# A fused attention and relu-squared MLP kernel: the second group's query and key loads wait for the first values load, and the first 185 steps stand in another order

## The chip, the cores and the metric

The kernel runs on one core of a Trainium2 chip. The metric is the device time of one execution in microseconds (us); before the change it is 211.09 us, the median of 3 runs (210.98 to 211.52). A core has five engines that each work through their own program in order: TensorE (PE in the profile; its weight loads are PEld), VectorE (DVE), ScalarE (ACT), GpSimd (POOL) and SyncE (SP), which here only issues DMAs.

## The reference

Attention over 4 batches of 8 heads, 768 tokens and 64 channels, in which each query sees the first 4 keys (the sinks) and the last 128 keys up to itself; then a two-layer MLP on the heads put side by side, 3072 tokens by 512 channels.

```python
keep = (pos[None, :] < n_sink) | ((rel >= 0) & (rel < window))
a = softmax(where(keep, q @ k.T / sqrt(D), -1e9))
x = (a @ v).transpose(0, 2, 1, 3).reshape(B * S, H * D)   # 3072 x 512
h = x @ w_in                                              # 512 x 2048
r = maximum(h, 0)
out = (r * r) @ w_out                                     # 2048 x 512
```

## The kernel before

Tokens lie in tiles of 128. Batch 0 is worked in three groups of two tiles: group 0 is tokens 0 to 255, group 1 tokens 256 to 511, group 2 the rest; the texts below call group 1 the second group. For a group, four loads bring keys and queries as fp32, 256 KB each: two for the keys and two for the queries, each for four heads (`m` = 0 or 2 counts pairs of heads). `load_qk` (L332, the DMA at L350) issues them on SP, but group 0's queries on ACT. From each load one **cast** makes bf16 (`qs<-qr`, in the helper `copy`: L192 on ACT, L194 on DVE). TensorE transposes it (`pt<-ident,qs`, L503), and one copy takes the result out of PSUM (`qkT<-pt`). Then come, per group, the scores (`ps`, L609; in group 0 with a matmul at L602 that adds the mask), the exponentials (`expm<-ps`, L630, ACT), the mask over the window's edges (L642 on DVE by a product with `tri`, or L218 on POOL by a select), the sinks' scores (`pk`, L568, and `es`, L576), the values product (`po`, L678), and the norm: a reciprocal and a product on DVE (L694, L695), two instructions for each quarter. The **bridge** turns the result over for the MLP (`px<-ident,xn_sb`, L727, copied to `xT`). **Layer 1** (L762) multiplies `xT` with w_in, four blocks of 128 columns at a time into PSUM `pm`; relu and square follow on ACT and DVE, and layer 2 later.

w_in is loaded in four quarters of 512 KB (`load_w_in`, L307), w_out in four too (L315), the values in tiles of 128 tokens, two to a call (`load_v`, L380, 128 KB a tile, converted on the way), group 2's and batch 1's keys and queries as bf16 (`load_cast`, L371). All of these are issued by POOL and go over one queue, q0 in the profile, which takes them in order of issue. SP's loads go over q1, ACT's over q10. `load_sinks` (L423) brings the sink tokens' values of one batch (8 KB) on SP, and POOL spreads them over heads once they are there (`vs<-vs_in,head_rows`, L550, four instructions).

Nothing in the kernel decides the order at run time. Every step is created as an `Op` with a number that counts up in the order of creation, and the text table `ORDER` lists these numbers in the order in which the steps are issued; a letter behind a number picks the engine (p, d, a, g for PE, DVE, ACT, POOL), and `+0` or `+1` picks one of the two PSUM pools. Each engine works its share of the list in that order. The numbers of the loads come from the list of load calls near the end of the kernel (L1289 to L1312), so a moved call changes the numbers of others.

`DUMMIES` gives some steps a number of **idle passes**: 128x128 matmuls of `ident` on itself (`warm`, L185), whose result the step's own passes overwrite, or at the start `pw<-tri` (`warmup`, L1372). Before the change they are 29 at the start, 31 and 24 ahead of two of group 0's transposes, and 3 or 4 at three later steps: 95 passes.

`behind` in a load call makes a load wait until another has landed (`after_dma`, L208). `yields` is a hint to the planner which made the table, and has no effect on the instructions.

Of the kernel before, what the change touches and what calls it, by code (L numbers as in the profile page):

```python
# [18 lines left out]


ORDER = """
990 1 0 2 7 8 9 10 11 12 13 14 15 16 17 18 56a 991+0 55d 61a 3 60d 57+1 62+0 19 20 59a 5 6 58d 4 65 63d 67+0 21 64a
75+1 69 89d 22 77 23 76+0 68+0 24 25 70 71+1 88d 73 93d 90+0 78 79+1 72 94a 81 74 83+0 92d 100+1 91a 80 102 82 95+0 66
97d 26 85 110+1 101+1 96d 103g 104 84d 98+0 27 86d 152+0 105g 99 112 111+0 153 114 115g 106+1 113d 28 29 116+1 108
160+0 107 117 154a 30 109 118 119 161 120+1 121a 31 122 168+1 123d 169 32 33 34 155a 170a 162d 172+1 331 164+0 176+0
171d 163a 165 35 166d 36 167d 156+1 173 157 177 174d 124+1 158a 37 38 125a 126d 39 180+1 127+0 332 133+1 181 129d 178a
128a 136 130+1 179d 282+1 182d 334 131 141+1 132+0 140+1 183d 283 40 144 142 137g 284 285 41 145d 159d 143d 134 146+1
135d 147 286 138+1 287 288 278 139 42 43 148+0 175a 150 149d 151d 289 44 279 184+1 290 185 193+0 280 281 200+0 201 291
194 45 204+1 196+0 202 46 203 205 198a 186 197 207a 293 206 187+0 199a 216+0+0 47 48 195a 217 49 188d 234+1+0 50 235
190+0 219 208+0 87 292 237 209 295 191 218 297+0 189 220 51 336 52 212 53 210a 294 211 255+0 252+1 254 299 298 256 54  # L30
253a 257 444 223+0+1 333 238d 445 192a 226 304 213 224 221+0 312 222 300 241+1+0 301 214+0 296 244 215 302 225 446
# [26 lines left out]
985 967d 969 983 984 989 986 988 987  # L58
"""
DUMMIES = {  # L60
    57: 31, 62: 24, 75: 4, 85: 3, 110: 4, 991: 29,
}


# [53 lines left out]
def kernel(  # L118
# [58 lines left out]
    def bank(slot, name, shape, dtype):  # L177

        return rooms[slot.pool][slot.room].tile(shape, dtype, name=name, tag=f"{slot.pool}{slot.room}")
# [105 lines left out]
    def dma_op(queue, name, run, us, behind=None, takes=(), yields=()):  # L285

        def go(e):
            ds = run(e)
            if behind is not None:
                for d in ds:  # L290
                    after_dma(d, loaded[behind])
            loaded[name] = ds[-1]
        o = op(-5, {queue: (0.9 if queue == "pool" else 0.5) + (0.3 if behind else 0.0)}, go, dma=us, takes=takes,
               follow=[chained[queue]] if queue in chained else (),
               after=[ops[behind]] if behind is not None else ())
        ops[name] = chained[queue] = o
        o.yields += [ops[y] for y in yields]
        o.follow += [ops[y] for y in yields]
        return o
# [3 lines left out]
    def load_w_in(i, behind=None, yields=()):  # L303
        c = slice(512 * i, 512 * i + 512)
        w_in_op[i] = dma_op(
            "pool", ("w_in", i),
            lambda e: [nc.gpsimd.dma_start(out=w_in_sb[:, i],  # L307
                                           in_=moe_w_in[:, c].rearrange("(a p) f -> p a f", p=128))],
            2.6, behind, yields=yields)
        w_in_op[i].margin = 0.4 + 0.4 * i  # L310
# [21 lines left out]
    def load_qk(b, m0, ti, g, pairs=2, behind=None, yields=()):  # L332


        t0, n = GROUPS[b][g]
        shares = 4 // pairs if n == 2 else 2 if pairs == 1 else 1
        half, share = m0 // pairs % shares, ("share", b, g, ti, m0 // (pairs * shares))
        if not half:
            qr_slot[share] = Slot("qr", 4 if n == 2 and pairs == 1 else 2)
        for m in range(m0, m0 + pairs):  # L340
            qr_slot[b, m, ti, g] = qr_slot[share]

        def run(e):
            if half == 0:
                qr_t[share] = bank(qr_slot[share], "qr", [128, shares * 2 * pairs, n * D], FP32)
            t = qr_t[share][:, 2 * pairs * half:2 * pairs * half + 2 * pairs, :]
            qr_t[b, "all", m0, ti, g] = t
            for m in range(m0, m0 + pairs):
                qr_t[b, m, ti, g] = t[:, 2 * (m - m0):2 * (m - m0) + 2, :]
            return [(nc.sync if ti or g else nc.scalar).dma_start(  # L350
                out=t,
                in_=(q, k)[ti][b, 2 * m0:2 * m0 + 2 * pairs, t0:t0 + 128 * n, :].rearrange(
                    "h (p t) d -> p h (t d)", t=n))]
        o = dma_op("sp" if ti or g else "act", ("qk", b, m0, ti, g), run, 16 * pairs * ROW[256 * n] + (0.7 if (b, m0, ti, g) == (0, 0, 0, 0) else 0.0), behind,
                   () if half else [qr_slot[share]], yields)
        for m in range(m0, m0 + pairs):
            ops["qk", b, m, ti, g] = o
# [18 lines left out]
    def load_v(b, s, behind=None, yields=()):  # L376

        for t in (2 * s, 2 * s + 1):
            def run(e, t=t):
                return [nc.gpsimd.dma_start(  # L380
                    out=v_sb[b % 2][:, t, :, 0:D],
                    in_=v[b, :, 128 * t:128 * t + 128, :].rearrange("h p d -> p h d"))]
            o = dma_op("pool", ("v", b, t), run, 0.9, behind if t == 2 * s else None, (), yields)
            o.after.append(c_rest if b else c_fill)
        ops["cast", b, s] = o
# [35 lines left out]
    def load_sinks(queue, b):  # L421
        eng = nc.scalar if queue == "act" else nc.sync
        dma_op(queue, ("vs_in", b), lambda e: [eng.dma_start(out=vs_in[:, b, 0:D], in_=v[b, :, 0:NSINK, :])], 0.1)  # L423
# [862 lines left out]
    NATURAL, TURNED, BIASED = (2, 3), (), 1  # L1286
    FAST = {1: ((0, 1), (2,)), 2: ((0,), (1, 2)), 3: ((0,), (1, 2))}
    CLASSIC2 = ((0, 0),)
    for g in range(2):  # L1289
        for m in (0, 2):  # L1290
            for ti in (1, 0):
                load_qk(0, m, ti, g)
            if m and not g:
                load_sinks("sp", 0)
    for b in range(1, B):
        load_sinks("sp", b)
    load_v(0, 0, None, [("qk", 0, 2, 0, 1)])
    load_w_in(0)
    load_v(0, 1)
    for i in range(1, 4):  # L1300
# [109 lines left out]
```

## Time and profile before

| | |
|---|---|
| median of 3 runs | 211.09 us |
| profiled execution | 209.94 us |
| its span, first to last instruction | 208.2 us |
| PE busy | 200.9 us (96%) |
| DVE busy | 178.0 us (85%) |
| ACT busy | 131.6 us (63%) |
| POOL busy | 98.6 us (47%) |
| q0, the software queue | 12.59 MB, 82.7% of 16 DMA engines' span |

All durations below are from the one profiled execution; microseconds count from the start of its span. A row of a timeline gives the start, the time that it takes, the engine, the line in the kernel, the operation with output and input, the shapes and the count of alike instructions; in brackets stands how long the engine was idle just before, and what ended that. "SPq" and "ACTq" are issues of DMAs on these engines. [...] A row of the table of stretches gives from:to, the length, the busy time of PE, PEld, DVE, ACT and POOL with the number of instructions, then the granted clock, the DMA share and the GB/s.

### The profile page before, as it was taken

The numbers are of one execution on the slowest core, as the hardware profiler recorded it, in microseconds if no ns is written. First come the engines' busy times: TensorE is split into PE (matmuls) and PEld (weight loads), VectorE is DVE, ScalarE is ACT, GpSimd is POOL, SyncE is SP. The second block draws the span as 40 slices with busy tenths as digits, with TensorE's granted clock in tenths as the row PEclk, the third lists the DMA queues.
The fourth block names the chain that finished last, engine by engine and source line by source line (L and its number), as shares of the span: only waits on it lengthen the run. The fifth ranks groups of instructions, "written<-read, shape, count | busy, mean of one in ns | idle before, by whom it ended". The sixth has DMA issues, their size and how long they took to land.

```text
span 208.2 us, 6087 instructions
## 1 busy us (share of the span) xinstructions
PE 200.9 (96%) x2535; PEld 177.6 (85%) x2535; DVE 178.0 (85%) x343; ACT 131.6 (63%) x205; POOL 98.6 (47%) x141
## 2 busy tenths in 40 slices
PE   7979999999899999999999999999999999999993
PEld 7757997579878889889878988998889999999893
DVE  5385767989999998999998888999989998998853
ACT  2678428718988168899888448989871452584010
POOL 7767983899489936989523529000280000000000
PEclk9999999999999999999999999999999999999999
DMA  5999999999999999999999995901023220200205
GB/s 162 218 216 202 184 186 213 177 155 179 148 61 118 156 137 241 92 188 154 129 138 229 108 136 152 159 0 25 4 50 127 57 82 22 101 0 3 99 5 201
DMA packets 96043, 26.12 MB, mean 125 GB/s; under 512 B 86800, under 2 KB 93456, under 8 KB 96016
## 3 DMA queue, kind: packets, MB, share of 16 engines
q0 software_dynamic: 69248, 12.59, 82.7%
q1 hardware_dynamic: 25568, 12.49, 28.6%
q10 hardware_dynamic: 1200, 0.66, 1.1%
q8 instruction: 20, 0.33, 0.6%
q14 instruction: 7, 0.06, 0.1%
HBM read 27.30 MB, written 6.29 MB: 161 GB/s over the span
## 4 chain that ended last, share of the span: by engine, by line
PE 76%; DVE 10%; DMA 6%; ACT 5%; issue 1%; ACTq 0%
PE py L1239 25%; PE pm L892 25%; PE pm L762 9%; DMA qr<-in_q_dram 6%; PE po L678 5%; PE ps L609 4%; PE py L990 3%; PE py L1100 2%; PE pt L503 1%; DVE sg L1213 1%; DVE xn_sb L695 1%; DVE r L942 1%; ACT gT_sb L915 1%; ACT qkT L192 1%; DVE gT_sb L1213 1%
## 5 line engine op out<-in xcount | busy, mean ns | idle before, releaser
L630 ACT ACTIVATE expm<-ps 128x1024 bf16<-128x1024 f32 (+1 forms) x48 | 44.1, 953 | 10.0 <-PE ps L609 8.9
L218 POOL TENSOR_SCALAR_AFFINE_SELECT expm<-expm 128x512 bf16<-128x512 bf16 x38 | 26.5, 730 | 46.9 <-ACT expm L630 21.5
L942 DVE CUSTOM_DVE_ANT_0 r<-pm,t 128x512 bf16<-128x512 f32 x54 | 36.0, 684 | 1.6 <-PE pm L892 1.2
L1239 PEld LDWEIGHTS <-gT_sb 128*128 128x128 bf16 x320 | 30.4, 98 | 4.5 <-issue 0.9
L892 PEld LDWEIGHTS <-w_in_sb 128*128 128x128 bf16 x384 | 32.5, 114 | 1.7 <-issue 1.5
L192 ACT ACTIVATE t<-pm 128x512 f32<-128x512 f32 x42 | 24.7, 600 | 13.4 <-PE pm L892 12.7
L192 ACT ACTIVATE osb<-py 128x256 f32<-128x256 f32 (+1 forms) x36 | 14.0, 397 | 19.9 <-PE py L1239 15.0
L892 PEld LDWEIGHTS <-wi 128*128 128x128 bf16 x288 | 24.7, 114 | 0.8 <-issue 0.7
L1239 PEld LDWEIGHTS <-sg 128*128 128x128 bf16 x240 | 22.5, 98 | 3.1 <-DVE sg L1213 0.3
L762 PE MATMUL pm<-xT,w_in_sb 128*128 128x256 bf16 x192 | 22.7, 273 | 0.4 <-DVE xT L194 0.4
L892 PE MATMUL pm<-xs,wi 128*128 128x256 bf16 (+1 forms) x192 | 21.6, 246 | 0.0
L892 PE MATMUL pm<-xs,w_in_sb 128*128 128x256 bf16 (+1 forms) x192 | 21.5, 246 | 0.0
L762 PEld LDWEIGHTS <-w_in_sb 128*128 128x128 bf16 x192 | 20.5, 114 | 1.1 <-issue 0.8
L1239 PE MATMUL py<-wt,gT_sb 128*128 128x256 bf16 x160 | 20.7, 273 | 0.2
L1239 PE MATMUL py<-wt,sg 128*128 128x256 bf16 x160 | 20.8, 273 | 0.0
L1239 PE MATMUL py<-w_out_sb,gT_sb 128*128 128x256 bf16 x160 | 20.4, 273 | 0.0
L915 ACT ACTIVATE gT_sb<-r 128x1024 bf16<-128x1024 bf16 x17 | 18.0, 1057 | 1.8 <-DVE r L942 1.6
L678 PE MATMUL po<-v,expm 128*128 128x65 bf16 x352 | 18.0, 193 | 0.5 <-ACT expm L630 0.3
L678 PEld LDWEIGHTS <-expm 128*128 128x128 bf16 x352 | 16.8, 97 | 1.8 <-ACT expm L630 0.5
L695 DVE TENSOR_TENSOR xn_sb<-po,rc 128x512 bf16<-128x512 f32 (+1 forms) x28 | 17.2, 615 | 1.0
L1253 DVE TENSOR_TENSOR osb<-py,osb 128x256 f32<-128x256 f32 x30 | 12.1, 415 | 4.7 <-PE py L1239 4.6
L609 PE MATMUL ps<-qkT 64*128 64x128 bf16 (+1 forms) x256 | 14.5, 238 | 0.9 <-ACT expm L630 0.6
(108 smaller groups left out, 382.2 us busy)
## 6 DMA issues: line engine op xcount, KB each, us to landing
out_dram<-osb SPq DMA_DIRECT2D x11, 512.0 KB, 3.4
v<-in_v_dram POOLq DMA_DIRECT2D x24, 128.0 KB, 6.3
qn<-in_k_dram POOLq DMA_DIRECT2D x20, 128.0 KB, 6.6
qn<-in_q_dram POOLq DMA_DIRECT2D x20, 128.0 KB, 6.2
w_in_sb<-in_moe_w_in_dram POOLq DMA_DIRECT2D x4, 512.0 KB, 9.4
w_out_sb<-in_moe_w_out_dram POOLq DMA_DIRECT2D x4, 512.0 KB, 10.0
qr<-in_k_dram SPq DMA_DIRECT2D x4, 256.0 KB, 6.8
qr<-in_q_dram ACTq DMA_DIRECT2D x2, 256.0 KB, 4.1
```

Of the source, the lines that this page charges most:

```text
L192: return nc.scalar.activation(out=dst, in_=src, func=AF.Copy)
L218: nc.gpsimd.affine_select(out=e_tile, in_=e_tile, compare_op=ALU.is_ge, fill=fill, base=i - 1, pattern=[[0, n], [1 if i else -1, 128]], ch ...
L609: nc.tensor.matmul(ps[:, h2, o:o + w], lhsT=qkT_sb[r, m, 1, c, :], rhs=qkT_sb[r, m, 0, qb:qb + w // 128, :], start=(i == 0 and not biased) ...
L630: nc.scalar.activation(out=x[:, :, o:512], in_=bank_t["s", b, s, m][:, :, o:512], func=AF.Exp, scale=scale)
L678: touch(("po", b, s, m0), e, nc.tensor.matmul(pv[:, i, h2, :], lhsT=lhsT, rhs=rhs, start=(n_ == 0), stop=(n_ == len(mms) - 1)), j)
L695: touch(("po", b, s, m0), e, nc.vector.tensor_tensor(out=xn_sb[:, 2 * s:2 * s + 2, 128 * (m0 + j0):128 * (m0 + j0 + nj)].rearrange("p i (j ...
L762: nc.tensor.matmul(pm[:, i, :], lhsT=w_in_sb[:, fb // 4, kb, fb % 4:512:4], rhs=xT[:, c0 // 256:(c0 + cw) // 256, kb, :], start=(kb == 0), ...
L892: touch(tag, e, nc.tensor.matmul(y[:, bk, i, :], lhsT=weights(name, f0 + i, a), rhs=rhs[:, a, :], start=fresh and i == 0 and a == 0, stop= ...
L915: nc.scalar.activation(out=d, in_=x, func=AF.Square)
L942: touch(tag, e, nc.vector._custom_dve(TENSOR_ADD_SAT, out=d.rearrange("p n c -> p (n c)"), in0=T["y"][:, 1].rearrange("p n c -> p (n c)"), ...
L1239: touch((b, u), e, nc.tensor.matmul(region(name), lhsT=x[:, i, :], rhs=w_[:, i, :], start=first and i == 0, stop=i == HB - 1, skip_group_c ...
L1253: ins = nc.vector.tensor_tensor(out=d, in0=region(of), in1=d, op=ALU.add)
```

## The change

Three things are edited. **The load list**: the four loads of group 1's keys and queries come after the first values load, and the first of them (keys, heads 0 to 3) is told to wait until the first values tile has landed (`behind=("v", 0, 0)`). The sink loads of all four batches thereby come ahead of them on SP. **The order**: 185 steps at the start of `ORDER` are listed in another order; everything after them is as before. **The idle passes**: 57 and 62 (ahead of group 0's transposes) get 9 and 14 instead of 31 and 24, others 3 to 5: 68 passes instead of 95.

```diff
 ORDER = """
-990 1 0 2 7 8 9 10 11 12 13 14 15 16 17 18 56a 991+0 55d 61a 3 60d 57+1 62+0 19 20 59a 5 6 58d 4 65 63d 67+0 21 64a
+990 1 0 2 7 8 9 10 11 56d 60a 55d 991+0 3 15 57+0 61d 62+1 16 59a 12 64d 13 14 17 18 19 20 5 67+1 6 75+0 58d 88d 89d
...
 DUMMIES = {
-    57: 31, 62: 24, 75: 4, 85: 3, 110: 4, 991: 29,
+    57: 9, 62: 14, 75: 4, 101: 4, 100: 3, 83: 5, 991: 29,
 }
...
-    for g in range(2):
-        for m in (0, 2):
-            for ti in (1, 0):
-                load_qk(0, m, ti, g)
-            if m and not g:
-                load_sinks("sp", 0)
+    for m in (0, 2):
+        for ti in (1, 0):
+            load_qk(0, m, ti, 0)
+    load_sinks("sp", 0)
     for b in range(1, B):
         load_sinks("sp", b)
-    load_v(0, 0, None, [("qk", 0, 2, 0, 1)])
+    load_v(0, 0)
+    for m in (0, 2):
+        for ti in (1, 0):
+            load_qk(0, m, ti, 1, behind=("v", 0, 0) if (m, ti) == (0, 1) else None)
     load_w_in(0)
```

The program of SP from its first row, before (`qr` are group 0's keys, then group 1's four loads; `DMAHW` is a landing of a hardware-queue load, `DMASW` one of the software queue):

```order
L350 DMA qr<-in_k_dram 128x4x128 x2
L423 DMA vs_in<-in_v_dram 32x1x64
L350 DMA qr<-in_k_dram 128x4x128
L350 DMA qr<-in_q_dram 128x4x128
L350 DMA qr<-in_k_dram 128x4x128
L350 DMA qr<-in_q_dram 128x4x128 [waits DMAHW0_49]
L423 DMA vs_in<-in_v_dram 32x1x64 [waits DMAHW1_49]
L423 DMA vs_in<-in_v_dram 32x1x64 [waits DMAHW2_49]
L423 DMA vs_in<-in_v_dram 32x1x64 [waits DMAHW3_49]
```

and of the change:

```order
L350 DMA qr<-in_k_dram 128x4x128 x2
L423 DMA vs_in<-in_v_dram 32x1x64 x4
L350 DMA qr<-in_k_dram 128x4x128 [waits DMAHW0_49,DMASW0_49]
L350 DMA qr<-in_q_dram 128x4x128 [waits DMAHW1_49]
L350 DMA qr<-in_k_dram 128x4x128 [waits DMAHW2_49]
L350 DMA qr<-in_q_dram 128x4x128 [waits DMAHW3_49]
L1013 DMA out_dram<-osb 128x1024 [waits DMAHW4_49,Activation_49]
```

Group 1's four loads moved behind the four sink loads, and the first of them now waits for DMASW0, the first values tile. The last row is the first store of an output tile, next on SP in both.

On DVE, the casts of group 1 and the norms of group 0 (`rc` and `xn_sb`), before; the fourth cast of group 1, of the queries of heads 4 to 7, is on ACT there:

```order
L194 CAST qs<-qr 128x512 [waits DMAHW6_49]
L194 CAST qs<-qr 128x512 [waits DMAHW5_49]
L194 CAST qs<-qr 128x512 [waits DMAHW7_49,DVE_49]
L694 RECIPROCAL rc<-po 128x4 [waits PE_49]
L695 TENSOR_TENSOR xn_sb<-po,rc 128x2x128 [waits DVE_49]
```

and the same place of the change, up to the masks of group 1 (`expm<-expm,tri`):

```order
L194 CAST qs<-qr 128x512 [waits DMAHW2_49]
L694 RECIPROCAL rc<-po 128x4 [waits PE_49]
L695 TENSOR_TENSOR xn_sb<-po,rc 128x2x128 [waits DVE_49]
L194 CAST qs<-qr 128x512 [waits DMAHW3_49]
L694 RECIPROCAL rc<-po 128x4 [waits PE_49]
L695 TENSOR_TENSOR xn_sb<-po,rc 128x2x128 [waits DVE_49]
L694 RECIPROCAL rc<-po 128x4
L695 TENSOR_TENSOR xn_sb<-po,rc 128x2x128 [waits DVE_49]
L194 COPY qkT_179<-pt 128x2x256 [waits PE_49]
L194 COPY xT_184<-px 128x512 [waits PE_49] x2
L642 TENSOR_TENSOR expm<-expm,tri 128x1024 [waits Activation_49,Pool_49]
L642 TENSOR_TENSOR expm<-expm,tri 128x1024 [waits Activation_49] x2
```

All four casts of group 1 are on DVE now, and norms of group 0 stand between them; the masks of group 1, of which POOL made some, follow on DVE.

On POOL, around the issues of the loads behind w_in, as a difference:

```order
 L380 DMA v_181<-in_v_dram 128x8x64 x2
 L307 DMA w_in_sb<-in_moe_w_in_dram 128x4x512 x3
-L218 AFFINE_SELECT expm<-expm 128x4x128 x2
-L371 DMA qn<-in_k_dram 128x8x64
-L218 AFFINE_SELECT expm<-expm 128x4x128 x4
-L371 DMA qn<-in_k_dram 128x8x64
+L371 DMA qn<-in_k_dram 128x8x64 x2
 L371 DMA qn<-in_q_dram 128x8x64 x2
 L380 DMA v_181<-in_v_dram 128x8x64 x2
```

POOL issues the same loads in the same order, and its six selects for group 1's masks no longer stand between them. Ahead of these rows POOL's program is the same in both: two values tiles, the selects that build the constants, the sink values (L550), the first quarter of w_in, two values tiles, three quarters of w_in.

More of the change, by code (lines that the diff above doesn't have):

```diff
@@ L21 @@
 ORDER = """
-990 1 0 2 7 8 9 10 11 12 13 14 15 16 17 18 56a 991+0 55d 61a 3 60d 57+1 62+0 19 20 59a 5 6 58d 4 65 63d 67+0 21 64a
[L23 to L28, printed above, removed]
+990 1 0 2 7 8 9 10 11 56d 60a 55d 991+0 3 15 57+0 61d 62+1 16 59a 12 64d 13 14 17 18 19 20 5 67+1 6 75+0 58d 88d 89d
+63a 69 4 65 76+1 77 78 68+0 21 79+0 71+1 80 90+1 93d 22 70 91a 81 92a 82 94d 73 74 101+0 66 23 72 104 24 100+1 95+0
+97a 25 96d 83+1 85 84d 98+0 26 86d 105d 27 102 103d 99 111+0 110+1 152+1 28 114 112 153 106+0 108 113d 115d 154a 109
+29 116+1 160+1 107 118 117 119 161 30 120+0 122 162d 31 168+1 123d 155a 121d 169 32 33 163a 164+1 34 170d 165 331 166a
+156+0 157 171d 332 172+1 176+1 124+1 35 158d 159a 173 125d 174a 127+1 177 167a 128d 129d 36 37 180+1 181 141+1 38 126d
+178d 39 144 40 140+0 282+0 182d 142 145d 283 133+0 136 132+0 41 143d 179d 130+1 183d 134 334 284 285 42 135d 137g 286
+131 138+0 43 139 146+0 287 147 175a 148+1 278 149a 288 44 150 151d 279 289 184+1 290 185 193+0 280 281 200+0 201 291
 194 45 204+1 196+0 202 46 203 205 198a 186 197 207a 293 206 187+0 199a 216+0+0 47 48 195a 217 49 188d 234+1+0 50 235
```

## The prediction

> **What bounds the kernel now.** I read the head of the page, then the chain of waits over the first 24 us, then each engine's timeline and the DMA landings there. The order of work after the first 185 steps is untouched, so only these microseconds can move the time.
>
> ```profile
> PE 200.9 (96%) x2535; PEld 177.6 (85%) x2535; DVE 178.0 (85%) x343; ACT 131.6 (63%) x205; POOL 98.6 (47%) x141
> PE 76%; DVE 10%; DMA 6%; ACT 5%; issue 1%; ACTq 0%
> ```
>
> TensorE is busy for 200.9 of 208.2 us: after the start it has hardly a gap, so the kernel ends earlier by what TensorE reaches the common part earlier, if nothing there was waiting already. The chain of waits at the start:
>
> ```profile
> 4.95 8.88 DMA qr<-in_q_dram
> ...
> 13.91 0.63 ACT qs L192
> 14.54 0.50 ACT qkT L192
> ...
> 15.07 0.40 PE pt L503 x4
> ...
> 15.49 1.29 DVE qkT L194 x2
> 16.78 0.67 DVE xT L194 x2
> ...
> 17.50 1.03 PE pm L762 x8
> ```
>
> The last load of the second group's queries is issued at 4.95 and lands 8.88 us later, at 13.82. Its cast, copy, transpose and copy follow one by one until TensorE takes up layer 1 at 17.50 and stays busy. Lost time of TensorE before that, by stretches (the first pair of numbers after the length is its busy time):
>
> ```profile
> 11.50:12.00 0.50, 0.39 (x8) 0.23 (x6) 0.33 (x1) 0.45 (x1) 0.50 (x2) 1.00 1.31 320
> 12.00:14.00 2.00, 1.45 (x33) 1.31 (x31) 1.87 (x7) 1.15 (x3) 1.96 (x3) 1.00 1.23 202
> 14.00:16.00 2.00, 1.32 (x22) 1.15 (x22) 1.58 (x6) 2.00 (x4) 0.00 (x0) 1.00 2.11 165
> 16.00:18.00 2.00, 1.65 (x27) 1.29 (x25) 1.44 (x4) 1.28 (x4) 1.93 (x3) 1.00 1.37 203
> 18.00:20.80 2.80, 2.80 (x56) 2.44 (x55) 1.20 (x3) 2.80 (x4) 2.03 (x5) 1.00 1.24 207
> ```
>
> Idle: 0.11 + 0.55 + 0.68 + 0.35 = **1.69 us**, and nothing from 18.0 on. The place that I measure at is the first pass over the second quarter of w_in, which I call the hinge; before it both orders hold the same useful passes, and behind it too.
>
> ```profile
> 20.78 1.04 PE L762 MATMUL pm<-xT,w_in_sb 128*128 128x256 bf16 x8
> ```
>
> Its weights, by POOL's timeline and by the landings of the two issues that begin from 11.71 and from 12.5 on (KB, then us to landing):
>
> ```profile
> 11.71 2.25 POOL L307 DMA_DIRECT2D w_in_sb<-in_moe_w_in_dram  x3
> ```
>
> ```profile
> w_in_sb<-in_moe_w_in_dram POOLq DMA_DIRECT2D x1, 512.0 KB, 8.5
> ```
>
> ```profile
> w_in_sb<-in_moe_w_in_dram POOLq DMA_DIRECT2D x1, 512.0 KB, 10.3
> ```
>
> TensorE gets there at 20.78. The second quarter, issued at 11.71, landed 8.5 us later, at 20.2: only 0.58 us of slack. The third (issued at about 12.5) landed 10.3 later, near 22.8. So the hinge has three limits: TensorE's own work, the second group's queries, and the software queue that brings w_in. I work out each.
>
> **Part 1: the loads.** First SP's timeline, then the landing of the first values tile, then the first 6 us of GB/s in 40 slices of 0.15 us:
>
> ```profile
> 5.36 3.52 SPq L423 DMA_DIRECT2D vs_in<-in_v_dram  x3
> ```
>
> ```profile
> v<-in_v_dram POOLq DMA_DIRECT2D x1, 128.0 KB, 6.8
> ```
>
> ```profile
> GB/s 0 0 0 0 0 0 0 0 0 0 0 0 3 157 212 140 24 34 65 205 348 341 335 355 345 338 348 338 341 328 290 290 297 290 280 294 297 283 279 222
> ```
>
> With hardware loads alone the chip moves about 340 GB/s from 3.0 us on: a load of 256 KB takes 0.77 us, four take 3.1, and I take 3.2. The first values tile, issued at 1.88, lands 6.8 us later, at 8.67. By queue (packets, MB, share) the stretches 5.4 to 6.0, 6.0 to 6.5 and 6.5 to 10 us show why:
>
> ```profile
> q0 software_dynamic: 81, 0.01, 26.9%
> ```
>
> ```profile
> q0 software_dynamic: 429, 0.05, 170.9%
> ```
>
> ```profile
> q1 hardware_dynamic: 1165, 0.58, 81.7%
> q0 software_dynamic: 1240, 0.16, 68.1%
> ```
>
> Its packets begin only shortly before 6.0 (81 of them), run at 429 in half a microsecond while the hardware queue is thin, and from 6.5 on take turns with the second group's loads one for one, 1165 against 1240. A tile is 1024 packets (128 tokens of 8 heads), so at the pace of the middle row it takes 1024/429 x 0.5 = 1.2 us. In the changed kernel the second group is not there yet: from about 5.9 on, the **first tile lands at about 7.1** (at best 6.8, with less sharing than that row still had; at worst 8.7, as now). SP waits for that landing, then issues four loads. The first load of all was issued at 0.82 and the GB/s row rises in the slice from 1.95 on: 1.15 us. So the second group's data are there at 7.1 + 0.05 + 1.15 + 3.2 = **11.5** (11.2 to 13.1 with the ends above), and the last landing, by the stragglers, by 12.4, instead of 13.82. Behind the waiting load SP holds only the three other loads; its next row is the first store, after 40 us. The sink loads, on SP until 8.88 in before, now go ahead.
>
> The software queue is worked in order of issue, and w_in stands behind the second tile. How much of w_in had moved before the hardware queue let go, from 11.2 to 11.7 and from 11.71 to 12.0:
>
> ```profile
> q0 software_dynamic: 21, 0.01, 12.2%
> ```
>
> ```profile
> q0 software_dynamic: 27, 0.03, 56.7%
> ```
>
> 0.04 MB, or 0.2 us at the 200 GB/s that the row 12.00:14.00 shows for w_in alone. So in before the stream has the engines as if from 12.0 - 0.2 = 11.8 on, now from 11.5: w_in comes **d = 0.3 us earlier** (ends +0.6 and -1.25). The hinge's weights then land at 20.2 - 0.3 = 19.9.
>
> **Part 2: the second group's path.** Its last cast is now on DVE, with a pair of norms ahead of it and of the cast before, where it was ACT's (0.63 us in the chain). What these take on DVE:
>
> ```profile
> 11.67 0.43 DVE L194 CAST qs<-qr 128x512 bf16<-128x512 f32 x1 [0.43 <-DMA qr<-in_k_dram]
> 12.10 0.18 DVE L694 RECIPROCAL rc<-po 128x4 f32<-128x4 f32 x1
> 12.32 0.42 DVE L695 TENSOR_TENSOR xn_sb<-po,rc 128x256 bf16<-128x256 f32 x1
> ```
>
> In before, from the landing at 13.82 to the hinge at 20.78 are 6.96 us; with 0.43 for 0.63 that is 6.75. Data at 13.2 would put the hinge at 19.95, level with the weights; data at 14.0 at 20.75, the time of before; each later microsecond costs one. At 12.4 it gives 19.15 and does not bind, and a norm pair of 0.6 us in front of the cast (19.75) doesn't make it bind either. The second group's masks go from POOL to DVE, some 0.7 us a tile; DVE is busy for 1.20 of 2.80 us in the row 18.00:20.80, so two tiles more fit there. Without that cover they would cost 0.7 each.
>
> **Part 3: TensorE's own work.** The idle passes:
>
> ```profile
> 1.27 3.27 PE L1372 MATMUL pw<-tri 128*128 128x128 bf16 x29 [1.27 <-DVE tri L224]
> 4.34 2.01 PE L185 MATMUL pt<-ident 128*128 128x128 bf16 x31
> 6.63 1.50 PE L185 MATMUL pt<-ident 128*128 128x128 bf16 x24
> ```
>
> From the second row on a pass takes 56 ns (24 x 56 = 1344 ns, the rest of the third row's 1.50 being the last one's way through the array). The 31 and 24 passes become 9 and 14: 32 fewer, 1.8 us. They stood where TensorE waited for loads anyway, so what goes is cover, not time, except where loads come sooner. Behind 8 us there were 4 + 3 + 4 = 11 by the table in the change, now 4 + 4 + 3 + 5 = 16: 5 x 56 ns = 0.28 us more, in gaps of the 1.69. So without data waits TensorE would be at the hinge at 20.78 - 1.69 = **19.1** at the soonest.
>
> **Sum.** Hinge = the latest of 19.1 (own work), 19.15 (second group) and 19.9 plus 0.1 for the wait's end (weights) = **20.0**. Against 20.78: **-0.78 us**. The third quarter, 22.8 - 0.3 = 22.5, is wanted at about 23.34 - 0.78 = 22.56, the row of layer 1 that begins at 23.34 in before: it just fits. On the profiled execution: 209.94 (1.7 us of which lie around the span) - 0.78 = 209.16. That execution stands 1.15 us below the median of the runs shown, 211.09, so I give 211.09 - 0.78 = **210.3**. The measurement tells apart about 0.3%, 0.63 us.
>
> [...] The 29 passes of the first row of Part 3 take from 1.27 to 4.34, 106 ns each, and the later ones 56: TensorE has two speeds at the start, though the granted clock in the windows reads 1.00 throughout. [...]
>
> **Rivals.**
>
> (a) *The software stream gains nothing.* The first values tile lands at 7.7 instead of 7.1, or the first of the four loads takes long to come up to speed, as the GB/s row does between 1.95 and 3.0. Then the data are there at 12.1, d = -0.3, weights 20.5, hinge 20.6: -0.2 us, **210.9**, within what can be told apart. For it: 0.6 us is less than the spread of my bounds. Against it: from 6.0 to 8.3 the engines have nothing but the two values tiles. Chance 0.26.
>
> (b) *Slower: the last second-group loads share.* The sink loads now land before 7 us and POOL's sink values no longer wait, so w_in's first quarter is issued sooner:
>
> ```profile
> 7.26 1.75 POOL L550 TENSOR_TENSOR vs<-vs_in,head_rows 32x130 bf16<-32x130 f32 x4 [1.35 <-DMA vs_in<-in_v_dram]
> 8.96 0.82 POOL L307 DMA_DIRECT2D w_in_sb<-in_moe_w_in_dram  x1
> ```
>
> POOL waited 1.35 us there; without it the issue is at 7.6. Its packets then take turns with the second group's for two or three microseconds, as v's did with q1 in the shared rows. If the last queries land at 15 instead of 12.4, the path of Part 2 gives 15 + 6.75 = 21.75 and the hinge is +0.97 us later; with some 0.15 given back by the idle of TensorE that is left, I put +0.8: **211.9**. It decides from a landing at 14.0 on. Against it: 1 MB at half of 340 GB/s takes 6.2 us, from 8.3 to 14.5, and the first quarter has packets for only some 2.5 us of that. The same time comes out when the first values tile lands at 8.7 as now (d = -1.25, weights 21.45, +0.67). Together chance 0.16.
>
> (c) *The clock falls.* Only 38 passes (29 + 9) now lie back to back: 1.27 + 29 x 0.106 + 9 x 0.056 = 4.85. The first transposes stood at 6.18 in before, so TensorE has some 1.2 us of idle there that it did not have. If that brings the slow pace back, each pass costs 107 for 56 ns until the clock returns: with 3 us of it, half of them useful passes, +1.5 us at most, and -0.15 if all of them fall into waits. Middle +0.7: **211.8**. Against it: the slow pace at the start ended after 3.07 us of work, and the 14 passes and the transposes follow at once. Chance 0.08.
>
> (d) *TensorE's own limit.* The weights land at 19.0, d above 0.6, the hinge at 19.1: -1.7 us, **209.4**. Chance 0.10.
>
> **How the numbers follow.** The forecast with its own spread (data at 11.2 to 11.8: -1.1 to -0.5) has 0.40. Range: from (d) 209.4 to the end of (b) 212.0. Faster by over 0.3%: 0.40 less the 0.04 of it under 0.63 us, (d) 0.10, and 0.04 of (a) and (c): 0.50. Slower: (b) 0.16, less what falls inside 0.63 us (0.02), and most of (c) 0.06: 0.20. The rest, 0.30, is within.
>
> **What would show it.** Right: vs_in's three loads off SP's wait, the first values tile at about 7.1, the last second-group query by 12.4, the second quarter of w_in at 19.9, TensorE's hinge at 20.0, and the rest of the trace shifted by the same 0.8. (a) shows in the values tile and w_in; (b) in a last query after 14.0 and TensorE waiting for its transposes; (c) in passes of 107 ns after 6 us. My forecast is wrong if TensorE waits anew behind the hinge, so that the 0.8 us are given back.

## The result, and the profile after

The changed kernel takes **217.66 us** (median of 4 runs, 216.01 to 219.36) against 211.12 us before (4 runs, 210.98 to 211.52): 1.028 times as long, 95% interval 1.0218 to 1.0343. Here and below medians are of all runs, while ratios and intervals leave out the slow ones, those over 1.5% above the fastest of the same kernel. The forecast was 210.3 us with a range of 209.4 to 212.0: wrong in sign, and far out of the range. The profiled execution took 218.01 us, with a span of 216.3 us, 8.1 us more than before's.

The page of the changed kernel, first the busy times, then the granted clock of TensorE in 40 slices of 5.4 us:

```profile
PE 203.4 (94%) x2506; PEld 177.9 (82%) x2508; DVE 180.6 (83%) x347; ACT 131.7 (61%) x204; POOL 95.5 (44%) x135
...
PEclk9995599999999999999999999999999999999999
```

TensorE is busy 2.5 us longer although it issues 29 matmuls fewer in the records, and the clock row has two slices at half speed that before had not. Both lie in the first 27 us. TensorE's timeline there, with the first useful pass over the second group's keys and queries, and the hinge:

```profile
10.85 0.54 PE L678 MATMUL po<-v,expm 128*128 128x65 bf16 x12
13.59 0.28 PE L503 MATMUL pt<-ident,qs 128*128 128x128 bf16 x2 [2.21 <-DVE qs L194]
...
18.31 0.40 PE L503 MATMUL pt<-ident,qs 128*128 128x128 bf16 x2 [1.27 <-DVE xn_sb L695]
20.11 0.82 PE L503 MATMUL pt<-ident,qs 128*128 128x128 bf16 x6 [1.41 <-DVE qs L194]
```

```profile
28.10 1.03 PE L762 MATMUL pm<-xT,w_in_sb 128*128 128x256 bf16 x8
```

The hinge is at 28.10, where it was at 20.78 before and was forecast at 20.0: **7.3 of the 8.1 us** are lost ahead of it. TensorE waits 2.21 us for the first casts and 1.27 + 1.41 us before the last; the 1.27 us end with a norm that the new order puts behind the third cast on DVE. DVE's own timeline says what those casts wait for:

```profile
12.77 1.50 DVE L194 CAST qs<-qr 128x512 bf16<-128x512 f32 x2 [3.68 <-DMA qr<-in_k_dram]
...
17.27 0.43 DVE L194 CAST qs<-qr 128x512 bf16<-128x512 f32 x1 [2.46 <-DMA qr<-in_k_dram]
...
19.23 0.81 DVE L194 CAST qs<-qr 128x512 bf16<-128x512 f32 x1 [0.99 <-DMA qr<-in_q_dram]
```

They are loads. SP's timeline, then the landing of the first values tile and of the last query load (issued at 9.87), the last number being the us from issue to landing:

```profile
8.34 0.39 SPq L350 DMA_DIRECT2D qr<-in_k_dram  x1
8.77 0.50 SPq L350 DMA_DIRECT2D qr<-in_q_dram  x1
9.32 0.51 SPq L350 DMA_DIRECT2D qr<-in_k_dram  x1
9.87 0.51 SPq L350 DMA_DIRECT2D qr<-in_q_dram  x1
```

```profile
v<-in_v_dram POOLq DMA_DIRECT2D x1, 128.0 KB, 6.4
```

```profile
qr<-in_q_dram SPq DMA_DIRECT2D x1, 256.0 KB, 9.3
```

The values tile lands at 1.88 + 6.4 = 8.3 and not at 7.1; the last query at 9.87 + 9.3 = 19.2 and not by 12.4. In before it was 13.82. A load that was issued 4.9 us later landed 5.4 us later, although the values no longer stood beside it.

### The profile page after: what moved, and what is told of

Same layout as the page of the kernel before. It is cut to its first block, busy times and chain, and to the rows that moved or that the text cites. A ratio compares the mean times of both kernels' runs of the same rounds, so it can differ in the third digit from the quotient of the medians.

```text
span 216.3 us, 6027 instructions
## 1 busy us (share of the span) xinstructions
PE 203.4 (94%) x2506; PEld 177.9 (82%) x2508; DVE 180.6 (83%) x347; ACT 131.7 (61%) x204; POOL 95.5 (44%) x135
## 3 DMA queue, kind: packets, MB, share of 16 engines
q1 hardware_dynamic: 25568, 12.49, 26.2%
## 4 chain that ended last, share of the span: by engine, by line
PE 62%; DMA 17%; DVE 10%; ACT 4%; issue 2%; POOL 1%; SPq 1%; ACTq 0%
PE py L1239 24%; PE pm L892 24%; DMA qn<-in_q_dram 6%; DMA qr<-in_q_dram 4%; DMA qn<-in_k_dram 4%; PE po L678 4%; PE ps L609 3%; DMA v<-in_v_dram 3%; PE pm L762 2%; PE py L1100 2%; DVE wi L811 1%; POOL qn L371 1%; PE py L990 1%; DVE expm L642 1%; DVE sg L1213 1%
## 5 line engine op out<-in xcount | busy, mean ns | idle before, releaser
L218 POOL TENSOR_SCALAR_AFFINE_SELECT expm<-expm 128x512 bf16<-128x512 bf16 x32 | 23.4, 765 | 46.5 <-ACT expm L630 20.4
L192 ACT ACTIVATE t<-pm 128x512 f32<-128x512 f32 x42 | 24.7, 600 | 13.4 <-PE pm L892 12.7
L192 ACT ACTIVATE osb<-py 128x256 f32<-128x256 f32 (+1 forms) x36 | 14.1, 398 | 15.9 <-PE py L1239 15.0
L762 PE MATMUL pm<-xT,w_in_sb 128*128 128x256 bf16 x192 | 23.5, 280 | 0.0
L695 DVE TENSOR_TENSOR xn_sb<-po,rc 128x512 bf16<-128x512 f32 (+1 forms) x28 | 17.2, 615 | 1.0
L609 PE MATMUL ps<-qkT 64*128 64x128 bf16 (+1 forms) x256 | 15.1, 245 | 0.6 <-ACT expm L630 0.5
```

Source lines behind the costliest of these rows:

```text
L192: return nc.scalar.activation(out=dst, in_=src, func=AF.Copy)
L218: nc.gpsimd.affine_select(out=e_tile, in_=e_tile, compare_op=ALU.is_ge, fill=fill, base=i - 1, pattern=[[0, n], [1 if i else -1, 128]], ch ...
L609: nc.tensor.matmul(ps[:, h2, o:o + w], lhsT=qkT_sb[r, m, 1, c, :], rhs=qkT_sb[r, m, 0, qb:qb + w // 128, :], start=(i == 0 and not biased) ...
L695: touch(("po", b, s, m0), e, nc.vector.tensor_tensor(out=xn_sb[:, 2 * s:2 * s + 2, 128 * (m0 + j0):128 * (m0 + j0 + nj)].rearrange("p i (j ...
L762: nc.tensor.matmul(pm[:, i, :], lhsT=w_in_sb[:, fb // 4, kb, fb % 4:512:4], rhs=xT[:, c0 // 256:(c0 + cw) // 256, kb, :], start=(kb == 0), ...
```

## The experiments

**Theory A**: the wait starts the second group's loads so late that they meet the first quarter of w_in on the DMA engines and take turns with it; TensorE stands idle, and as a second part its clock falls. **Theory B**: the new order with its fewer idle passes loses the time by itself.

### The change without its wait

```diff
-            load_qk(0, m, ti, 1, behind=("v", 0, 0) if (m, ti) == (0, 1) else None)
+            load_qk(0, m, ti, 1)
```

> The change with its order, its idle passes and its load list, but the second group's first load no longer waits for the first values tile. Theory A (the wait starts the second group's loads at 8.34 us, so that they meet the first quarter of w_in on the DMA engines and the last lands at 18.86; TensorE stands idle and loses its clock): the loads are issued from about 4.9 us on, behind the four sink loads, the last query lands at 13 to 14 us, the hinge is at 20 to 20.8 us, 210.3 to 211.3 us in all. Theory B (the new order of the steps and the 27 passes fewer lose the time by themselves): 216 to 218 us as with the change.

Measured: 210.74 us against 210.9 (ratio 0.9982, interval 0.9955 to 1.0009). The last query, issued at 7.33, landed 5.0 us later, at 12.3, and TensorE's hinge:

```profile
19.94 1.07 PE L762 MATMUL pm<-xT,w_in_sb 128*128 128x256 bf16 x8 [0.49 <-DMA w_in_sb<-in_moe_w_in_dram]
```

It waits for the second quarter of w_in, landed at 19.9. B falls: order, load list and passes together are no loss. The hinge comes 0.84 us sooner than in before, yet the span is only 0.4 us shorter (207.8); the last run comes back to that.

### The old order and passes with the wait

The kernel before with the change's load list and wait; in the order only the moved loads change places.

> The kernel before with its order of compute steps and its 95 idle passes, but with the load list and the wait of the change. Theory A: the last query lands at 18 to 19 us as with the change, TensorE waits for it, 215.5 to 218 us. Theory B: the loads alone cost little, 210.5 to 212 us.

Measured: 217.3 us (ratio 1.027, interval 1.0218 to 1.0321), within 0.4 us of the change. Its profiled execution was an outlier of 221.21 us, so no row of it is read. With the change's load list, the wait makes the loss in either order.

### The change, waiting for another load

```diff
+            ... behind=("qk", 0, 2, 0, 0) if (m, ti) == (0, 1) else None)
```

> The change with one other thing to wait for: the second group's first load waits for the last query load of the first group (landed at 6.97 us) and not for the first values tile (8.32). Theory A, with w_in's packets as the cause: the loads begin 1.35 us sooner, the most of their data is through before the first packets of w_in at 11.8 us, the last query lands at 12 to 13.5 us, the hinge is at 20 to 20.3 us, 210.3 to 210.7 us. If waiting for any landing is what costs, whatever follows: a last query near 17.5 us and about 216 us.

Measured: 212.81 us (ratio 1.0101, interval 1.0044 to 1.0159): between the two figures. The loads began at 6.99, the last was issued at 8.51 and landed 5.9 us later at 14.4, later than the 12 to 13.5 expected. The second quarter of w_in came late too, at 21.9, which was in neither expectation, but it did not set the hinge: TensorE reached it at 22.38 without a wait. From the landing to the hinge it took 8.0 us, where before took 6.96; the clock was at 0.50 from 16.4 to 19.8. By the ratios, a wait that ends 1.35 us sooner leaves a loss of 1.0%, where the change has 2.8%.

### The change, with w_in behind the second group's loads

```diff
-    load_w_in(0)
+    load_w_in(0, ("qk", 0, 2, 0, 1))
```

> The change, with its wait, and in addition the first quarter of w_in (with all the loads that follow it on POOL's queue) waits until the last query load of the second group has landed. Theory A (w_in's packets on the shared engines delay the second group's loads): the loads are issued at about 8.1 to 9.8 us as in the change, but the last one lands at 12.5 to 13.5 us and not at 18.9. The w_in stream then starts about 3 us later than in the kernel before, its second quarter lands near 23.3 us and sets the hinge at 23.5 us: 213.5 to 214.5 us. If something else makes the loads slow after the wait: the last query at 17 us or later, and over 218 us, since w_in comes later still.

Measured: 216.47 us (ratio 1.0286 of 210.44, interval 1.0237 to 1.0335). The last query's landing (issued at 9.69) and the hinge:

```profile
qr<-in_q_dram SPq DMA_DIRECT2D x1, 256.0 KB, 4.2
```

```profile
24.23 1.04 PE L762 MATMUL pm<-xT,w_in_sb 128*128 128x256 bf16 x8
```

With nothing beside it the load takes 4.2 us instead of 9.3 and lands at 13.9: **the software queue's packets, w_in's first of all, are what made it slow.** The two values tiles behind w_in's first quarter were held back with it; the next run tells the two apart. The hinge came 0.7 us behind the time expected, after a wait of 1.47 us for w_in's first quarter and with the clock at 0.50 from 20.3 to 23.8; the total is 2 us above what was expected. In the profiled execution TensorE lost another 0.64 us to w_in behind the hinge, 0.5 us to group 2's last mask and 1.0 us at 135.6 us to a DMA transpose of batch 2; w_in's late stream is no cure.

### The change, with two values tiles ahead of w_in

```diff
-    load_w_in(0)
     load_v(0, 1)
+    load_w_in(0)
```

> The change, with its wait, but the third and fourth values tile are issued ahead of the first quarter of w_in, so that the second group's loads share the engines with packets of 128 bytes (32 ns each) for the first 2 us and not with packets of 1 KB (96 ns). If it is turns, packet by packet, that make the loads slow, their pace goes by the other queue's packet: next to values about 340 packets a microsecond as in the kernel before, next to w_in 110 to 135. 2048 packets are to move; some 900 go before the other queue begins, 700 beside the values, the rest beside w_in: the last query lands at 14.5 to 16 us instead of 17.5 to 19, and the time is 213 to 215.5 us. If the sharing alone counts, whoever shares: 17.5 to 19 us again and 217 us.

Measured: 213.66 us (ratio 1.0115 of 211.04, interval 1.0051 to 1.0178). The last query, issued at 9.68, took 6.2 us and landed at 15.9, both as expected of turns. The pace by queue (packets, MB, share of 16 engines), from 14 to 15 us in the change, beside w_in:

```profile
q0 software_dynamic: 140, 0.14, 87.1%
q1 hardware_dynamic: 110, 0.06, 26.8%
```

and from 13 to 14 us in this run, beside values:

```profile
q0 software_dynamic: 414, 0.05, 80.8%
q1 hardware_dynamic: 294, 0.15, 71.9%
```

A packet of w_in takes 0.871 x 16 / 140 = 100 ns by these rows, one of the values 0.808 x 16 / 414 = 31 ns, one of the second group 39 ns in both. If a turn is one of each, it takes 139 ns beside w_in, which is 115 turns in a microsecond on 16 engines, and 110 packets of the second group were counted. Beside values a turn is 70 ns, 229 turns, but 294 packets were counted: the shares sum to 153%, so packets overlap there, and the sum of the two times is too long a turn. The order of the paces is as turns have it; their sizes only roughly. Alone the queue moved this much, from 10 to 11 us in the change:

```profile
q1 hardware_dynamic: 626, 0.31, 104.1%
```

So the same load goes at 110, 294 or 626 packets a microsecond, according to who shares the engines. The counts are roughly one for one: 140 against 110 packets in that microsecond beside w_in, while the bytes are 0.14 against 0.06 MB, and 414 against 294 beside values. That an engine takes the packets of the two queues in turn is my reading of these counts; no view here shows the packets of a single engine.

### The change with its idle time filled

Two runs: 56 idle passes ahead of the second group's last transposes, then 30; 40 ahead of its first in both.

```diff
-    57: 9, 62: 14, 75: 4, 101: 4, 100: 3, 83: 5, 991: 29,
+    57: 9, 62: 14, 75: 4, 90: 40, 101: 4, 100: 3, 95: 56, 83: 5, 991: 29,
```

> The change with 40 more idle passes ahead of the second group's first transposes and 56 more ahead of its last, in the time in which TensorE stands idle. Theory A with the clock as a second part (the granted clock falls to half from 16.0 to 26.2 us because of the idle time): the clock stays at 1.00, the hinge comes at 18.86 + 6.75 = 25.6 us in place of 28.1, 215.2 us, 2.4 less than the change. If the clock counts for nothing and TensorE only waits for data: 217.6 us again, or more by the passes that stick out.

Measured with 56: 218.75 us (215.35 to 221.11 in 4 runs, ratio 1.0256, interval 1.018 to 1.0332), no gain that can be told from the change. In the profiled execution the last query landed at 17.4 and the hinge was at 25.09, 7.65 us behind it: the clock stayed up, at 1.00 from 6 to 22 us, but the passes stuck out.

> As in the run with filled idle time, but with 30 passes and not 56 ahead of the second group's last transposes, so that none sticks out behind the data (40 stay ahead of the first). If the idle time's clock costs about 2.3 us: the clock stays near 1.00, the hinge comes 6.8 to 7.3 us after the last query's landing in place of 9.2, and the median is 1.5 to 2.4 us below that of the change on the same chip. If the clock counts for nothing: the same median as the change.

> The change once more, unaltered, to see how far its times and the landing of the last query vary: 216 to 219.5 us, the last query between 17 and 19.5 us.

Measured on one chip: 215.35 us with 30 passes (214.17 to 217.51 in 6 runs), 218.01 us for the change again (214.74 to 218.3 in 5 of 6 runs, one at 237.46). The medians are 2.7 us apart, but by the ratios to before, 1.0234 (1.0186 to 1.0283) for the filled one and 1.028 (1.0224 to 1.0337) for the change, it is only 1.0 us, and the intervals overlap: the times alone show no gain. The profiled executions show what the clock costs on the way to the hinge. In the change's second one the last query landed at 18.9, as expected, and the hinge was at 27.25. The filled kernel's rows of two stretches, and its hinge:

```profile
12.00:14.00 2.00, 2.00 (x40) 2.00 (x38) 0.70 (x3) 0.00 (x0) 2.00 (x4) 1.00 1.11 188
...
16.00:18.00 2.00, 0.94 (x17) 0.95 (x18) 0.96 (x4) 0.63 (x1) 0.52 (x1) 1.00 2.03 177
```

```profile
24.63 1.03 PE L762 MATMUL pm<-xT,w_in_sb 128*128 128x256 bf16 x8
```

The clock (third number from the end) stays at 1.00. The last query was issued at 9.45 and landed 8.5 us later, at 17.96; from there to the hinge are 6.7 us. In the change it was 28.10 - 19.2 = 8.9, in before 6.96. So the half clock costs some **2 us** on that path. The other profiled executions line up with this: 7.7 us (values first) and 8.0 us (waiting for the first group) with 3.4 us at half clock behind the landing, 8.4 us with 6.1 us of it (the change again). In the change the clock fell here:

```profile
15.60:16.00 0.40, 0.32 (x6) 0.19 (x6) 0.00 (x0) 0.40 (x2) 0.18 (x1) 0.99 1.13 205
16.00:16.40 0.40, 0.39 (x3) 0.21 (x2) 0.00 (x0) 0.36 (x3) 0.00 (x0) 0.50 1.28 220
25.60:26.00 0.40, 0.40 (x4) 0.27 (x3) 0.35 (x1) 0.02 (x1) 0.09 (x1) 0.50 1.23 205
...
26.40:26.60 0.20, 0.20 (x4) 0.20 (x2) 0.20 (x1) 0.00 (x0) 0.06 (x1) 1.00 1.62 182
```

from 16.0 to about 26.2 us, three times 3.4 us. The longest idle stretch ahead of that was 2.21 us.

### The kernel before with fewer idle passes

```diff
-    57: 31, 62: 24, 75: 4, 85: 3, 110: 4, 991: 29,
+    57: 9, 62: 14, 75: 4, 85: 3, 110: 4, 991: 29,
```

> The kernel before with nothing changed but the idle passes ahead of the first group's two transposes: 9 and 14 for 31 and 24, as in the change. Theory A: they lay beside waits for loads, and the clock does not fall, since the idle stretches that they leave are about 1 us: 210.4 to 211.2 us, the same as before within 0.3%. If fewer passes cost the clock at the start: the granted clock under 1.00 before 16 us and 212 us or more.

Measured: **209.7 us** (209.38 to 210.46 in 10 runs) against 211.04: ratio 0.995, interval 0.9923 to 0.9976. Faster, which the theory did not say, and the best of all versions here. TensorE's timeline in this run:

```profile
4.24 0.67 PE L185 MATMUL pt<-ident 128*128 128x128 bf16 x9
5.19 0.28 PE L503 MATMUL pt<-ident,qs 128*128 128x128 bf16 x2 [0.29 <-DVE qs L194]
...
20.26 1.04 PE L762 MATMUL pm<-xT,w_in_sb 128*128 128x256 bf16 x8
```

The first transposes start at 5.19; in before, the 31 passes held TensorE to 6.18. The hinge is 0.52 us sooner. In the profiled pair the last query also landed sooner (12.4), so not all of the 0.52 us need come from the passes; the ratio of the runs is what carries the verdict.

### The change without its wait, and one sum later

```diff
-178d 39 144 40 140+0 282+0 182d 142 145d 283 133+0 136 132+0 41 143d 179d 130+1 183d 134 334 284 285 42 135d 137g 286
-131 138+0 43 139 146+0 287 147 175a 148+1 278 149a 288 44 150 151d 279 289 184+1 290 185 193+0 280 281 200+0 201 291
+178d 39 144 40 140+0 282+0 182d 142 145d 283 133+0 136 132+0 41 143d 179d 130+1 183d 134 284 285 42 135d 137g 286
+131 138+0 43 139 146+0 287 147 175a 148+1 278 149a 288 44 150 151d 334 279 289 184+1 290 185 193+0 280 281 200+0 201 291
```

> The change without the wait, and one vector operation listed later: the sum over w_in's columns that stood on DVE ahead of group 2's last mask now stands behind the norms. In the run without the wait the hinge came 0.84 us sooner than in the kernel before, but TensorE then waited 0.52 us for that mask at 40 us. If that wait is where the gain went: TensorE keeps some 0.8 us, 0.4 us less than without the wait alone, 210.0 us against 210.9. If another wait takes its place: 210.5 us again.

In the run without the wait, this row stood where the gain went:

```profile
40.48 0.24 PE L678 MATMUL po<-v,expm 128*128 128x65 bf16 x2 [0.52 <-DVE expm L642]
```

It is the last mask of group 2, which the new order puts behind a sum over w_in on DVE. With the sum moved, this wait was gone and TensorE stayed 0.7 to 0.8 us ahead of before up to 129 us. Then another took its place in the profiled execution:

```profile
130.09 0.40 PE L568 MATMUL pk<-qkT,kblk 128*32 128x512 bf16 x4 [0.98 <-DMA qkT<-qn]
```

Measured: 210.83 us against 210.44 (ratio 0.9993, interval 0.9963 to 1.0023): no difference. Why that DMA transpose is late in some executions stays open; it cost 1.0 to 1.2 us also in the runs that waited for the first group and with w_in behind the second group's loads, and in the change's second profiled execution, and nothing in before's or the change's first.

## Why the prediction was wrong, point by point

**What bounds the kernel: right in the main.** The time moved by what the hinge moved: 7.3 of 8.1 us in the profiled pair. The rest contains the 0.5 us wait for group 2's last mask, which stands in the changed kernel's profile too. That only the first microseconds can move the time was too strong: this wait, and in some executions that for the DMA transpose, came anew far behind the hinge.

**The first tile "lands at about 7.1": wrong by 1.2 us.** On the whole the packets went as worked out; the software queue in the changed kernel, from 5 to 7 us:

```profile
q0 software_dynamic: 1084, 0.14, 107.6%
```

As many packets as a tile has, 1024, had gone by 7.0. What the sum left out is what lies between that and the landing. In the trace 16 packets of 4 bytes stand at the end of each tile's packets; the first tile's were taken from 6.73 to 7.33, and the landing came at 8.3, 1.0 us behind the last of them. In before that gap was 0.3 us (8.33 and 8.67). Why it was longer here stays open. My own bounds, 6.8 to 8.7, held the 8.3.

**The second group's data "at 11.5", landing "by 12.4": the step that failed.** The four loads were given 3.2 us at 340 GB/s, as if nothing shared the engines with them. That pace held only while the queue was alone. Two loads were nearly through when w_in came at about 11.8, and landed at 12.7 and 13.6; the other two crawled and landed at 17.2 and 19.2. The run without the wait landed the last query at 12.3 and its second quarter of w_in at 19.9, the hinge at 19.94: the numbers that I gave for the kernel with the wait. So the sum was that of another kernel, in which the loads are not held back.

**w_in "0.3 us earlier": wrong.** It landed later, since it shared the engines too; its second quarter in the changed kernel, issued at 11.76:

```profile
w_in_sb<-in_moe_w_in_dram POOLq DMA_DIRECT2D x1, 512.0 KB, 11.3
```

That is 23.1 us. It did not bind only because the queries were later still.

**TensorE's own work and the passes: half right.** In before's trace a pass starts 56 ns after the one ahead of it from 4.6 us on, and its record lasts 219 ns, which is what the row of 24 passes holds beyond their steps. The passes that went were no loss, as said, but no mere cover either: in before's own order, taking them away is worth 0.5%.

**Rival (b)** had the mechanism, w_in's first quarter sharing the engines with the last loads. Its reason for it was wrong: w_in was not issued sooner, since POOL still waited ahead of the sink values, and the issue stood at 9.21, where before had 8.96:

```profile
7.47 1.79 POOL L550 TENSOR_TENSOR vs<-vs_in,head_rows 32x130 bf16<-32x130 f32 x4 [1.37 <-DVE qs L194]
9.21 0.81 POOL L307 DMA_DIRECT2D w_in_sb<-in_moe_w_in_dram  x1
```

The second group's loads came later, and so met it. Its deciding point, a landing after 14.0, agrees with the runs, without being tested alone: landings at 14.4, 15.9 and 19.2 have hinges at 22.4, 23.6 and 28.1, but the clock fell in all three. Its size was wrong: I priced a landing at 15 and dismissed more, because "the first quarter has packets for only some 2.5 us". That took w_in's time alone. At the 140 packets a microsecond counted from 14 to 15, its 512 packets of 1 KB last 3.7 us; in the change they took from 11.8 to 18.0, with the slow microseconds from 12 to 14 among them. The landing of the last query was 19.2.

**Rival (c)** had the clock, at the wrong place: not the idle time after the first passes, which left it at 1.00 (in the run without the wait TensorE has 1.4 us of it, and its mean clock is 1.00), but the 2.21 us wait for the second group's casts and the broken work that followed. So the loss is (b) and (c) together, not one of them: the late load left TensorE about half idle (1.78 us of work from 12.58 to 15.99), and it then went on with the clock at 0.50. Of the 7.3 us at the hinge, 5.4 are the landing and 1.9 the slower path behind it (8.9 for 6.96 us).

**Rival (d)** needs weights at 19.0 for its 1.7 us, which is d = 1.2 and not the 0.6 given beside it. No run came near it.

## What to carry to other kernels

Before holding a load back, ask what will be on the same engines when it starts: price it by the packets of both queues and not by its bytes alone. Here its queue moved 626 packets a microsecond alone, 294 beside values and 110 beside w_in. The load that landed late cost twice, since TensorE starved: 5.4 us in the landing and 1.9 us behind it, with the clock at 0.50. Idle passes that keep the clock up must end when the data come: from the landing to the hinge it took 7.65 us with 56 of them ahead of the last transposes and 6.7 us with 30. The cheapest gain here was to have 32 fewer in the kernel before, worth 0.5%.

## What the runs showed of the hardware that was not expected

Two queues together went below the pace that the sum of turns gives, 115 packets of each in a microsecond beside w_in. The change from 13 to 14 us:

```profile
q0 software_dynamic: 64, 0.07, 43.0%
q1 hardware_dynamic: 93, 0.05, 20.8%
```

The engines' shares sum to 64%, although both queues had work; in the microsecond after, 140 and 110 packets moved. The run without the wait shows no such stretch, and neither does the change's second profiled execution (79.9% and 25.0% in the same microsecond), whose last query still landed at 18.9: the late landing does not rest on it. What held the engines there stays open.

TensorE's clock fell to half behind broken work: 2.21 us idle up to 13.59, then passes with shorter waits between them (0.46 us the longest), then 0.50 from 16.0 on. It stayed there for 10.24 us. In other runs here the half clock lasted 3.4 us (waiting for the first group, values first, w_in behind) or 6.8 us (the change again), so the lengths stand about as 1, 2 and 3 times 3.41 us.

The share of work in a stretch of that length is what the runs point to. The stretches here are cut in steps of 3.41 us from the times at which the clock record of each trace changes. The one before the fall in the change, and two that follow each other in the run with values first (the number behind the comma is TensorE's busy time):

```profile
12.58:15.99 3.41, 1.78 (x30) 1.39 (x31) 1.92 (x4) 1.11 (x3) 3.20 (x4) 1.00 0.95 162
```

```profile
10.91:14.32 3.41, 2.19 (x46) 1.71 (x42) 1.71 (x4) 1.85 (x4) 3.41 (x6) 1.00 1.24 198
14.32:17.73 3.41, 1.90 (x28) 1.13 (x23) 3.17 (x9) 2.59 (x6) 2.55 (x4) 1.00 1.57 192
```

Behind 2.19 us of work in 3.41 us the clock stayed, behind 1.90 and 1.78 us it fell. It also fell behind 0.48 us (the change again), 1.53 us (waiting for the first group) and 1.87 us (w_in behind), and stayed behind 2.00 us (without the wait) and 2.34 us (30 passes). So in the first 30 us of these runs it fell behind stretches with up to 56% of work and stayed with 59% or more. That is no firm threshold: near the end of the run with 30 passes a stretch with 48% left the clock at 1.00.
